# Window attention and two feed-forward layers: another hand-written order for the opening, and raw q and k pieces spaced wider

## The chip, the cores and the metric

The kernel runs on one core of one Trainium2 chip. The metric is the device time of one execution in microseconds (us), as the median of several runs; lower is better. Shares, waits and durations come from one execution that the hardware profiler took. The engines are PE (TensorE, with PEld for its weight loads), DVE (VectorE), ACT (ScalarE), POOL (GpSimd) and SP (SyncE, which issues most DMAs).

## The reference, cut to what matters

```python
# attention: batch 4, 8 heads, sequence 576, head size 64, a causal window of 64
scores = scale * np.matmul(q, k.transpose(0, 1, 3, 2))
mask = (rel >= 0) & (rel < 64)            # rel = row position - column position
attn = softmax(np.where(mask, scores, -1e9))
x = (attn @ v)                            # laid out as 2304 tokens x 512
h = np.maximum(np.maximum(x @ w1, x @ w2), x @ w3)   # 512 -> 768, three weights
x = h @ w_out                             # 768 -> 512
h = x @ w_in                              # 512 -> 2048
g = np.where(h >= 1, h, np.where(h <= -1, 0.0, (h + 1) ** 2 / 4))
out = g @ w2_out                          # 2048 -> 512
```

## The kernel before, in words

**The stages.** Attention and the first feed-forward product (stage A) run together, then come the second product (B), the third (C) and the fourth (D). Every fp32 matrix product of these layers is made of three passes over operands that are split into a high and a low part. Stages B to D use Strassen's seven products. The weights lie in memory as 64-bit words, from which two 32-bit halves are joined.

**Stage A.** The 2304 tokens are 9 blocks of 256. A product, named A0, A1 and so on, is one block times one 128-column piece of one of w1, w2, w3: 12 matmuls of 128x256 into one PSUM tile (`a_mm`, L427). `a_end` (L438, named D0, D1 and so on) takes the tile away: w1's on ACT, w2's and w3's with a maximum on DVE. After w3's in the second half of the columns, DVE makes sums (H) and SP stores `hq` (ST, `h_store` L456). There are 162 products. Before the 19th one, A12 to A17 take products of block 0 and block 1 in turn.

**Attention** goes by 36 groups g of 64 rows (`BL`), 9 to a batch. Its steps have short names, with n the group or, for loads and transposes of q and k, the pair of groups 2n and 2n+1:

- LQn, LKn: loads of q and k (`load`, L235), 256 KB each, or two halves where a batch ends. LVn: load of v (`vload`, L266).
- TQn, TKn: transposes on PE (`prep_t`, L282). CQn on ACT and CKn, the copies out of PSUM (`prep_c`, L287). 
- QKn: scores on PE. Rna, Rnb: mask and minimum on DVE (`red`, L342). Ena, Enb: exponentials on ACT (`ex`, L353). Sn: reciprocal on DVE (`norm`). Nn: scaling on POOL (`scale`, L371). PTn: transpose of the probabilities on PE (`ptr`). PCn: copy (`ptc`, L386). PVn: times v (`pv`, L393). VHn, VLn: high part on ACT and low part on DVE of the block's x (`values`, L405).

From group 18 on, except 26 and 27, q and k come in raw pieces (`raw_load`, L254): 16 pieces of 32 KB for q and 16 for k hold four groups, in rows of 32 numbers, and DVE transposes them.

**Weights of stage A** come in 9 pairs of 1 MB (LWn, `w_first` L638, `w_load` L165), two DMAs each, in 3 buffers `wst` (`NW`, L23). W1.n and W0.n are the two words on ACT (`w_word` L182, `w_lower` L199), SHn a shift on DVE (`w_upper`, L203), ADn the sum on DVE (`w_sum`, L207), HIn the high part (`w_high`, L211), LOna and LOnb the low parts on POOL (`w_low`, L214). Pair n holds the weights of A(2n) and A(2n+1) in the first 13 products. A `wst` buffer is free again after HIn and ADn. The decoded words have two buffers (`WT`, L24), held until LOnb.

**What sets the order.** Each engine and SP's queue work their instructions off in program order. Up to A17 that order is written out by hand in the string `SEQ` (L59), which `early` (L667) turns into steps. Steps before A0 stand in the order in which they are to go; later ones carry a place behind "@", counted in products. A star puts CQ, PC and HI on DVE and not on ACT; for CK it is the other way round (L665, L677). Steps from product 18 on and everything of the later groups get places from formulas (L689 to L716): a visit to two groups each 9 products, at place `vq`, with loads of q and k 13 products ahead of it (`LP - 4`), v at it, transposes 3 ahead. Raw pieces begin 28 products ahead (`RAWS`, L40), one each `RAWSTEP` of a product (L41, L702). The visits of groups 8, 10, 12 and 14 are at places 12.2, 18.2, 24.2 and 34.2. All places are sorted into one order (L803). PSUM tiles of TQ, TK and A share three buffers (L151).

```python
if g in pet:
    if g > g0:                                            # g0 = 8
        put(vq + LP - 4, load, g)
elif g in raws[::CH]:
    for z in range(32):
        put(vq + RAWS + RAWSTEP * z, raw_load, g, z)
put(vq, vload, g)
```

From place 14 on, a weight pair of the later stages is loaded, decoded, summed and stored each 6.2 products (`SLOTSTEP`, L55).

Of the kernel before, what the change touches and what calls it, by code (L numbers as in the profile page):

```python
# [37 lines left out]
STAGES = (-21, -9, -3, 0, 0.2, 1, 6, 9)  # L38
LP = -9
RAWS = -28  # L40
RAWSTEP = 0.4  # L41

# [12 lines left out]


SEQ = (  # L59
# [16 lines left out]
)  # L76
WS = 8

# [2 lines left out]
def kernel(ctx, tc, q, k, v, w1, w2, w3, wo1, wi2, wo2, out, hd, x2d, td, gd):  # L81
# [36 lines left out]
    N1 = max(n for _, n in blocks1)  # L118
# [508 lines left out]
    def put(at, fn, *args):  # L627
        order.append((at, len(order), fn, args))
# [60 lines left out]
    g0 = blocks1[PB][0] // BL  # L689
# [3 lines left out]
    for x, g1 in enumerate(range(g0, NG, 2)):  # L693
        vq, vt, vp = (visits[x + y] + 0.2 for y in range(3))
        for y in range(2):
            g = g1 + y
            if g in pet:
                if g > g0:
                    put(vq + LP - 4, load, g)
            elif g in raws[::CH]:  # L700
                for z in range(32):
                    put(vq + RAWS + RAWSTEP * z, raw_load, g, z)  # L702
            put(vq, vload, g)
            if g not in pet or g > g0:
                put(vq + STAGES[2], prep, g)
            if g > g0 + 1:
                put(vq + 0.02, qk, g)
                for z in range(2):
                    put(vq + RED[y] + z, red, g, (2 * z, 2 * z + 1))
                    put(vq + EXP[y] + z, ex, g, (2 * z, 2 * z + 1))  # L710
                put(vq + EXP[y] + 2, norm, g)
                put(vq + EXP[y] + 2, scale, g)
            put(vt + 0.01, ptr, g)
            put(vt + PTC[y], ptc, g)
            put(vp, pv, g)
        put(vp + 0.04, val, g1, 2)  # L716
# [365 lines left out]
```

## Time and profile before

| what | us |
|---|---|
| median of 3 runs | 772.27 (771.88 to 773.39) |
| the profiled execution, its own time | 770.42 |
| its span, first to last instruction | 768.6 |
| PE busy | 738.3 |
| DVE busy | 574.6 |
| ACT busy | 423.3 |
| POOL busy | 258.2 |

Two numbers on each engine are to be read together: its busy time, and what ended the idle time ahead of an instruction. PE's matmuls are counted busy at either level of its clock, so a matmul that takes twice as long is busy all that time; the granted clock stands in a column of its own. The mean granted clock over the span is 0.987 of full speed.

### The profile page before, as it was taken

The numbers are of one execution on the slowest core, as the hardware profiler recorded it, in microseconds if no ns is written. First come the engines' busy times: TensorE is split into PE (matmuls) and PEld (weight loads), VectorE is DVE, ScalarE is ACT, GpSimd is POOL, SyncE is SP. The second block draws the span as 40 slices with busy tenths as digits, with TensorE's granted clock in tenths as the row PEclk, the third lists the DMA queues.
The fourth block names the chain that finished last, engine by engine and source line by source line (L and its number), as shares of the span: only waits on it lengthen the run. The fifth ranks groups of instructions, "written<-read, shape, count | busy, mean of one in ns | idle before, by whom it ended". The sixth has DMA issues, their size and how long they took to land. (4 is left out here: it accounts for less than half of the span.)

```text
span 768.6 us, 17450 instructions
## 1 busy us (share of the span) xinstructions
PE 738.3 (96%) x6680; PEld 720.6 (94%) x6680; DVE 574.6 (75%) x1315; ACT 423.3 (55%) x806; POOL 258.2 (34%) x315
## 2 busy tenths in 40 slices
PE   5689999999999899999999999999999999999997
PEld 4578989999999799999999999999999999999997
DVE  4776767787786785677876778768888999988881
ACT  7865575556563553434547766767776434433330
POOL 2653395355535362300039442732269000000000
PEclk9798999999999999999999999999999999999999
DMA  9984989998999983797868653555456544544421
GB/s 247 288 232 115 232 193 259 252 326 206 257 248 278 332 256 121 229 296 227 246 185 286 203 146 122 201 188 196 162 199 190 170 138 144 167 126 123 130 83 55
DMA packets 221652, 154.75 MB, mean 201 GB/s; under 512 B 95233, under 2 KB 213633, under 8 KB 221569
## 3 DMA queue, kind: packets, MB, share of 16 engines
q1 hardware_dynamic: 191600, 110.91, 52.4%
q10 hardware_dynamic: 26384, 28.06, 10.4%
q0 software_dynamic: 3584, 14.68, 5.1%
q8 instruction: 52, 0.85, 0.5%
q14 instruction: 32, 0.25, 0.1%
HBM read 98.24 MB, written 55.38 MB: 200 GB/s over the span
## 5 line engine op out<-in xcount | busy, mean ns | idle before, releaser
L433 PE MATMUL ps<-xt,arena 128*128 128x256 f32 x1944 | 239.2, 284 | 8.3 <-DVE hq L450 3.5
L433 PEld LDWEIGHTS ps<-xt,arena 128*128 128x128 f32 x1944 | 233.3, 191 | 12.3 <-DVE hq L450 3.8
L125 ACT ACTIVATE side<-plain 128x1024 fp32r<-128x1024 f32 (+3 forms) x64 | 61.6, 978 | 56.9 <-DVE plain L504 36.8
L125 ACT ACTIVATE arena<-plain 128x1024 fp32r<-128x1024 f32 (+3 forms) x62 | 60.0, 977 | 35.7 <-DVE plain L504 25.8
L504 DVE TENSOR_TENSOR plain<-plain 128x256 f32<-128x256 f32 (+1 forms) x172 | 76.1, 459 | 4.7 <-DMA plain<-g_scratch 2.4
L128 DVE TENSOR_TENSOR side<-plain,side 128x1024 fp32r<-128x1024 f32 (+3 forms) x53 | 60.8, 1173 | 18.2 <-ACT side L125 18.2
L128 POOL TENSOR_TENSOR arena<-plain,arena 128x256 fp32r<-128x256 f32 (+1 forms) x65 | 54.6, 873 | 47.1 <-ACT arena L125 47.0
L128 POOL TENSOR_TENSOR side<-plain,side 128x256 fp32r<-128x256 f32 (+1 forms) x38 | 34.5, 942 | 101.6 <-ACT side L125 95.5
L125 ACT ACTIVATE ht<-ps 128x256 f32<-128x256 f32 x54 | 20.6, 382 | 79.8 <-PE ps L433 50.9
L360 ACT ACTIVATE sm<-sm,nm 128x128 f32<-128x128 f32 (+1 forms) x144 | 55.4, 392 | 15.4 <-DVE nm L348 14.7
L374 POOL TENSOR_TENSOR sm<-sm,rs 128x512 f32<-128x512 f32 (+1 forms) x36 | 37.4, 1041 | 57.6 <-DVE rs L369 50.8
L504 DVE TENSOR_TENSOR hq<-hq 128x128 f32<-128x128 f32 x108 | 55.4, 514 | 1.6
L450 DVE TENSOR_TENSOR ht<-ps,ht 128x256 f32<-128x256 f32 x54 | 22.7, 421 | 31.1 <-PE ps L433 17.0
L874 ACT ACTIVATE ut<-ut 128x288 f32<-128x288 f32 x64 | 43.9, 686 | 2.0
L128 DVE TENSOR_TENSOR arena<-plain,arena 128x1024 fp32r<-128x1024 f32 (+3 forms) x34 | 40.5, 1198 | 5.6 <-ACT arena L125 5.3
L450 DVE TENSOR_TENSOR hq<-ps,ht 128x256 f32<-128x256 f32 x54 | 22.5, 417 | 24.9 <-PE ps L433 19.4
L185 ACT ACTIVATE wst<-wst 128x1024 f32<-128x1024 f32 x28 | 32.1, 1147 | 14.1 <-DMA wst<-in_moe_w 7.3
L883 DVE SCALAR_TENSOR_TENSOR ut<-ut,evt 128x864 f32<-128x864 f32 x32 | 37.9, 1184 | 1.5 <-ACT ut L874 1.4
L128 POOL TENSOR_TENSOR arena<-wt,arena 128x512 fp32r<-128x512 f32 (+1 forms) x26 | 29.8, 1168 | 27.3 <-DVE wt L209 19.9
L504 POOL TENSOR_TENSOR wx<-wt 128x256 f32<-128x256 f32 x26 | 19.2, 740 | 57.7 <-DVE wt L197 50.0
L859 DVE TENSOR_TENSOR evt<-cc,evt 128x288 f32<-128x288 f32 x64 | 29.2, 456 | 8.4 <-PE cc L776 6.6
L125 ACT ACTIVATE evt<-ca 128x288 f32<-128x288 f32 x40 | 16.2, 405 | 34.0 <-PE ca L776 28.7
(170 smaller groups left out, 1779.5 us busy)
## 6 DMA issues: line engine op xcount, KB each, us to landing
g_scratch<-ut ACTq DMA_DIRECT2D x64, 288.0 KB, 3.1
plain<-g_scratch SPq DMA_DIRECT2D x36, 512.0 KB, 4.1
plain<-t_scratch SPq DMA_DIRECT2D x16, 896.0 KB, 5.3
h_scratch<-hq SPq DMA_DIRECT2D x27, 448.0 KB, 5.2
plain<-h_scratch SPq DMA_DIRECT2D x12, 1008.0 KB, 7.2
wst<-in_moe_w_out SPq DMA_DIRECT2D x22, 512.0 KB, 6.1
wst<-in_moe_w SPq DMA_DIRECT2D x18, 512.0 KB, 5.8
wst<-in_moe_w_in SPq DMA_DIRECT2D x16, 512.0 KB, 5.3
```

The costliest lines, as they stand in the source:

```text
L125: nc.scalar.activation(dst, src, AF.Copy, scale=scale)
L128: eng.tensor_tensor(dst, a, b, op=ALU.subtract)
L185: nc.scalar.activation(w.bitcast(F32), w.bitcast(F32), AF.Prelu, scale=2.0 ** (WS - 119), alpha=2.0 ** 32)
L360: nc.scalar.activation(sm[:, p, 0:W], sm[:, p, 0:W], AF.Exp, bias=d["nm"][:, p:p + 1], scale=-1.0, accum_out=ss[:, p:p + 1])
L374: nc.gpsimd.tensor_tensor(sm[:, :, 0:W], sm[:, :, 0:W], rs.unsqueeze(2).to_broadcast([P, NP, W]), op=ALU.mult)
L433: nc.tensor.matmul(ps[:, 0:n], w_col((w, f), wl, kt), xt[:, xl, kt, 0:n], start=(x == 0), stop=(x == len(passes) - 1))
L450: nc.vector.tensor_tensor(t[:, 0:n], ps[:, 0:n], part[j, f][:, 0:n], op=ALU.max)
L504: eng.tensor_tensor(o, a, b, op=op)
L859: nc.vector.tensor_tensor(o, a, b, op=ALU.add)
L874: nc.scalar.activation(o, o, AF.Square)
L883: nc.vector.scalar_tensor_tensor(o, o, 2.0 ** WS, x, op0=ALU.min, op1=ALU.max)
```

## The change

`SEQ` is replaced by another list of the same steps, with six more loads in it: LV8, LV9, LQ5, LK5, LQ6 and LK6, which the formulas gave places before. The formulas leave those six out now. In the list, LK4 stands ahead of A0 and not at place 8.25, LQ4, LV5 and LV6 behind A0, LW1 and LW2 further forward, and LW6 to LW8 at 5.78, 6.84 and 8.2, ahead of LV8, LQ5, LQ6, LK6 and LV9. W0.3 and W1.4 come ahead of A0; TQ4, CQ4, R6, R7b, E6a and E7a come behind it. CK0, CK3, CK4 go from ACT to DVE; PC0 and PC2 go from DVE to ACT, as do HI0, HI3 and HI8. `RAWSTEP` is 0.56 and not 0.4.

```diff
--- before.py
+++ after.py
@@ -38,7 +38,7 @@
 STAGES = (-21, -9, -3, 0, 0.2, 1, 6, 9)
 LP = -9
 RAWS = -28
-RAWSTEP = 0.4
+RAWSTEP = 0.56
 
 
 
@@ -57,22 +57,23 @@
 
 
 SEQ = (
-    "LQ0 LK0 TQ0 LQ1 CQ0 TK0 LK1 *CK0 TQ1 QK0 LK2 CQ1 QK1 R0a LQ2 TK1 E0a R0b R1a E0b TK2 LW0 CK1 E1a TQ2 S0 QK2 R1b "
-    "N0 CQ2 QK3 E1b R2a PT0 E2a R2b LV1 CK2 E2b *PC0 LV2 QK4 W0.0 S1 PV0 S2 LW1 N1 W1.0 R4a R3a N2 PT1 E3a R3b R4b "
-    "QK5 E3b SH0 E4b PT2 S3 LV3 *HI0 W0.1 AD0 LV4 W1.1 LQ3 *PC1 LO0a E4a *PC2 PV1 LK3 VH0 SH1 TQ3 N3 R5a LV5 HI1 TK3 "
-    "R5b LO0b S4 LW2 PT3 VH1 VL0 E5a VL1 PV2 N4 *PC3 CQ3 *CK3 AD1 PT4 VH2 E5b QK6 LQ4 VL2 LO1a W1.2 S5 PV3 R6a LW3 "
-    "W0.2 N5 TQ4 R6b QK7 E6a SH2 PT5 CQ4 LO1b R7a HI2 R7b LV6 AD2 E7a LW4 VH3 LO2a W1.3 VL3 "
-    "A0@0 E6b@0.19 SH3@0.33 E7b@0.74 LO2b@0.83 S6@0.9 A1@1 LW5@1.26 D0@1.29 S7@1.45 W1.4@1.56 N6@1.73 A2@2 PC4@2.33 "
-    "*HI3@2.47 W0.3@2.75 D1@2.98 N7@2.98 A3@3 D2@3.25 W0.4@3.3 LV7@3.3 AD3@3.42 PT6@3.58 W1.5@3.74 PV4@3.77 SH4@3.92 "
-    "A4@4 LW6@4.01 D3@4.32 *PC5@4.36 LO3a@4.36 PC6@4.59 A5@5 HI4@5.01 SH5@5.2 AD4@5.57 HI5@5.68 PT7@5.75 A6@6 "
-    "*PC7@6.21 LO3b@6.21 W1.6@6.23 LW7@6.31 D4@6.55 PV5@6.72 LO4a@6.86 D5@6.88 D6@6.92 A7@7 VH5@7.28 W0.5@7.55 "
-    "H5a@7.71 A8@8 LO4b@8.12 D7@8.24 LK4@8.25 W1.7@8.43 VL5@8.49 AD5@8.88 A9@9 W0.6@9.04 H5b@9.32 VH4@9.37 LW8@9.38 "
-    "TK4@9.44 D8@9.51 LO5a@9.51 D9@9.56 VL4@9.64 *CK4@9.71 PV6@9.83 SH6@9.91 A10@10 VH6@10.2 LO5b@10.2 HI6@10.4 "
-    "VL6@10.5 PV7@10.72 AD6@10.85 W1.8@10.94 A11@11 D10@11.36 W0.7@11.37 LO6a@11.43 QK8@11.54 D11@11.69 QK9@11.75 "
-    "VH7@11.78 R8a@11.89 A12@12 ST5@12 LO6b@12.01 VL7@12.1 E8a@12.24 R8b@12.39 E8b@12.84 SH7@12.9 A13@13 D12@13.39 "
-    "AD7@13.54 HI7@13.66 A14@14 H11a@14.4 D13@14.41 W0.8@14.68 LO7a@14.84 R9a@14.84 A15@15 R9b@15.29 E9a@15.44 "
-    "D14@15.6 LO7b@15.89 S8@15.9 E9b@15.98 A16@16 D15@16.28 H11b@16.79 A17@17 N8@17.23 D16@17.28 S9@17.58 SH8@17.96 "
-    "*HI8@17.98 AD8@17.98 D17@17.98 LO8a@17.98 LO8b@17.98 N9@17.98 ST11@18"
+    "LQ0 LK0 LQ1 LK1 LW0 LV1 TQ0 LV2 LK2 CQ0 TK0 LV3 LQ2 CK0 TQ1 LW1 QK0 CQ1 LW2 QK1 R0a LV4 TK1 E0a R0b R1a E0b CK1 "
+    "E1a S0 QK2 W1.0 R1b N0 QK3 E1b SH0 PT0 W0.0 S1 R3a N1 PC0 R2a TK2 R3b E3a AD0 PT1 E3b PV0 E2a S3 TQ2 *PC1 N3 VH0 "
+    "CK2 HI0 PV1 VL0 R2b CQ2 LO0a LW3 VH1 QK4 E2b LQ3 VL1 LO0b QK5 LK3 W1.1 S2 LK4 R4a W0.1 N2 R4b R5a E4b R5b PT2 "
+    "SH1 W0.2 PT3 AD1 E5b HI1 E4a LO1a LW4 *PC3 PC2 E5a S4 PV2 LO1b W1.2 S5 TQ3 N4 PV3 W0.3 SH2 TK3 CQ3 N5 TK4 VH2 "
+    "CK3 PT4 VH3 HI2 AD2 PT5 QK6 W1.3 QK7 VL3 LO2a LW5 VL2 W1.4 R7a "
+    "A0@0 LQ4@0.09 SH3@0.33 LV5@0.48 E7a@0.57 LO2b@0.82 R7b@0.82 A1@1 CK4@1.13 D0@1.28 HI3@1.55 AD3@1.72 A2@2 "
+    "W0.4@2.3 SH4@2.59 A3@3 E7b@3.06 D1@3.08 LO3a@3.08 D2@3.53 HI4@3.61 AD4@3.98 A4@4 D3@4.27 W1.5@4.48 LO3b@4.64 "
+    "S7@4.64 TQ4@4.75 D4@4.97 A5@5 LK5@5.01 CQ4@5.28 LV6@5.39 SH5@5.43 W0.5@5.71 LW6@5.78 N7@5.92 R6a@5.92 A6@6 "
+    "D5@6.28 LV7@6.45 E6a@6.47 R6b@6.58 LO4a@6.66 LW7@6.84 A7@7 HI5@7.02 AD5@7.56 D6@7.77 A8@8 E6b@8.01 D7@8.15 "
+    "LO4b@8.15 LW8@8.2 PC4@8.21 S6@8.26 *PC5@8.36 PV4@8.4 N6@8.46 D8@8.53 PV5@8.58 VH4@8.64 LO5a@8.72 PT6@8.77 "
+    "VL4@8.78 VH5@8.81 PT7@8.88 W1.6@8.91 VL5@8.96 A9@9 H5a@9.17 PC6@9.5 *PC7@9.6 LO5b@9.6 W0.6@9.92 A10@10 LV8@10.01 "
+    "LQ5@10.22 SH6@10.29 D9@10.39 LQ6@10.44 PV6@10.56 H5b@10.56 HI6@10.64 LK6@10.66 PV7@10.78 AD6@10.81 LV9@10.87 "
+    "A11@11 W1.7@11.07 D10@11.3 LO6a@11.38 VH6@11.5 QK8@11.56 W0.7@11.65 VL6@11.73 QK9@11.78 SH7@11.89 A12@12 ST5@12 "
+    "VH7@12.13 LO6b@12.29 R9a@12.29 HI7@12.42 VL7@12.59 D11@12.86 A13@13 AD7@13.16 D12@13.24 E9a@13.51 A14@14 "
+    "H11a@14.02 W1.8@14.06 LO7a@14.46 R9b@14.46 R8a@14.77 D13@14.83 A15@15 E8a@15.23 H11b@15.37 E9b@15.78 D14@15.81 "
+    "LO7b@15.81 A16@16 R8b@16.1 W0.8@16.33 S9@16.48 SH8@16.78 A17@17 E8b@17.03 D15@17.09 N9@17.09 D16@17.18 HI8@17.2 "
+    "AD8@17.32 D17@17.59 LO8a@17.63 S8@17.68 N8@17.92 ST11@18 LO8b@18.15"
 )
 WS = 8
 
@@ -695,12 +696,13 @@
         for y in range(2):
             g = g1 + y
             if g in pet:
-                if g > g0:
+                if g > g0 + 4:
                     put(vq + LP - 4, load, g)
             elif g in raws[::CH]:
                 for z in range(32):
                     put(vq + RAWS + RAWSTEP * z, raw_load, g, z)
-            put(vq, vload, g)
+            if g > g0 + 1:
+                put(vq, vload, g)
             if g not in pet or g > g0:
                 put(vq + STAGES[2], prep, g)
             if g > g0 + 1:
```

## Rows read from the trace of the kernel before

**Rows 1.** The page's part 1: busy time, share of the span, instructions.
```profile
PE 738.3 (96%) x6680; PEld 720.6 (94%) x6680; DVE 574.6 (75%) x1315; ACT 423.3 (55%) x806; POOL 258.2 (34%) x315
```

**Rows 2.** Windows: PE, PEld, DVE, ACT, POOL busy (instructions), granted clock, DMA share, GB/s.
```profile
0.00:10.00 10.00, 5.67 (x60) 4.44 (x64) 2.14 (x18) 4.85 (x14) 1.63 (x11) 1.00 0.89 217
10.00:20.00 10.00, 4.88 (x92) 3.38 (x92) 8.22 (x42) 9.61 (x33) 2.83 (x4) 1.00 1.19 272
20.00:30.00 10.00, 7.57 (x83) 6.11 (x84) 7.72 (x28) 6.91 (x21) 7.27 (x7) 0.66 1.01 261
...
40.00:50.00 10.00, 10.00 (x106) 9.57 (x105) 9.11 (x11) 7.93 (x11) 5.93 (x4) 1.00 0.69 205
50.00:60.00 10.00, 7.03 (x55) 6.33 (x54) 6.00 (x11) 5.18 (x9) 2.55 (x2) 0.76 1.00 285
...
250.00:260.00 10.00, 6.61 (x60) 6.48 (x62) 6.85 (x16) 3.80 (x12) 3.97 (x6) 0.83 1.06 308
```

**Rows 3.** Waits of PE, 0 to 150 us: total us, times, longest.
```profile
PE ps L433 <- ACT xt L125: 2.9, 1, 2.9
...
PE tp L285 <- DMA nat<-in_k: 2.2, 1, 2.2
...
PE ops L401 <- DVE xt L128: 0.8, 1, 0.8
```

**Rows 4.** PE's timeline, 25 to 110 us: start, us, what, [idle before <-releaser].
```profile
34.43 7.72 PE L433 MATMUL ps<-xt,arena 128*128 128x256 f32 x48 [2.94 <-ACT xt L125]
...
42.52 0.69 PE L401 MATMUL ops<-pt,vr 128*64 128x64 f32 x16
...
48.63 4.51 PE L433 MATMUL ps<-xt,arena 128*128 128x256 f32 x36
...
57.20 1.12 PE L401 MATMUL ops<-pt,vr 128*64 128x64 f32 x16 [0.80 <-DVE xt L128]
58.25 2.93 PE L433 MATMUL ps<-xt,arena 128*128 128x256 f32 x12
```

**Rows 5.** SP's timeline, 0 to 150 us: LW7, then LK4.
```profile
46.96 1.02 SPq L170 DMA_DIRECT2D wst<-in_moe_w  x2
48.02 1.88 SPq L249 DMA_DIRECT2D nat<-in_k  x2
```

**Rows 6.** DMA issues of 48 to 49 us: size, us to landing.
```profile
nat<-in_k SPq DMA_DIRECT2D x1, 128.0 KB, 6.6
```

**Rows 7.** Groups by form, 0 to 120 us: count | busy us, mean ns | idle before.
```profile
L360 ACT ACTIVATE sm<-sm,nm 128x128 f32<-128x128 f32 x56 | 21.8, 394 | 6.7 <-DVE nm L348 6.7
L374 POOL TENSOR_TENSOR sm<-sm,rs 128x512 f32<-128x512 f32 x13 | 14.8, 1142 | 15.0 <-DVE rs L369 10.5 <-DVE ss L368 4.4
...
L185 ACT ACTIVATE wst<-wst 128x1024 f32<-128x1024 f32 x12 | 13.8, 1150 | 7.3 <-DMA wst<-in_moe_w 7.3
...
L125 ACT ACTIVATE ht<-ps 128x256 f32<-128x256 f32 x14 | 5.3, 376 | 12.0 <-PE ps L433 12.0
...
L125 ACT ACTIVATE qt<-tp 128x512 f32<-128x512 f32 x8 | 4.7, 590 | 5.9 <-PE tp L285 5.8
```

**Rows 8.** Timeline, 25 to 62 us: a low part on POOL.
```profile
29.78 1.27 POOL L128 TENSOR_TENSOR arena<-wt,arena 128x512 fp32r<-128x512 f32 x1
```

**Rows 9.** Line 205 (SH), 30 to 62 us: duration ns minimum/median/maximum.
```profile
L205 DVE TENSOR_SCALAR wst<-wst x5: 685/1195/1543, 30.1 to 57.1; 128x1024 int32<-128x1024 int32 x5
```

**Rows 10.** PE's timeline, 240 to 300 us.
```profile
253.39 5.96 PE L433 MATMUL ps<-xt,arena 128*128 128x256 f32 x36 [3.45 <-DVE hq L450]
```

**Rows 11.** Line 457 (h_store): who waited for it, and landing min/median/max.
```profile
  DVE hq L450: 5.4, 1
...
DMA to landing us min/median/max: 3.3/5.2/9.6
```

**Rows 12.** SP's timeline, 225 to 262 us: raw k pieces, then the store.
```profile
237.21 4.88 SPq L260 DMA_DIRECT2D raw<-in_k  x7
...
243.20 0.56 SPq L457 DMA_DIRECT2D h_scratch<-hq  x1
```

## The prediction, made before the run

> **What bounds the kernel now.** I read four views, from the coarse to the fine. The engines' busy times come first: PE is busy for 738.3 of 768.6 us [rows 1], so a change that leaves the matmuls alone can win only PE's 30 us of idle time and what a lower clock costs. The windows say where that lies [rows 2]: in the first 30 us PE is busy 5.67, 4.88 and 7.57 us of each 10, from 40 to 50 all the time, from 50 to 60 only 7.03 at a granted clock of 0.76, and from 250 to 260 only 6.61 at 0.83. The waits name what ended the gaps [rows 3]: the first product waited 2.9 us for ACT; a transpose waited 2.2 us for a k load, and the PV after it 0.8 us. The timeline prices them [rows 4]: A0 starts at 34.43, and its first four products take 7.72 us where 36 matmuls, three products, take 4.51 at full clock, so part of them ran at the lower level (1.2 and not 2.4 GHz), right after 2.94 idle us. The same happens after the k load: the next product takes 2.93 us and not 1.50, and a PV 1.12 and not 0.69.
>
> **The k load's stall: 5.7 us.** In the order of before LK4 stands at place 8.25, behind LW7, and TK4 at 9.44. SP issued LW7 at 46.96 and LK4 at 48.02 [rows 5]; that kind of load took 6.6 us to land [rows 6], so at 54.6 or later, while PE had come to TK4 at 53.1 (48.63 + 4.51 [rows 4]). The idle time is 2.2 + 0.8 = 3.0 us, which is what the window of 50 to 60 lacks. The lower clock costs 2.93 - 1.50 = 1.4 for the product and 1.12 - 0.69 = 0.4 each for the transpose and two PVs, together 2.7. In the new list LK4 stands ahead of LW4 and TK4 ahead of A0, so this goes: -5.7 us. What is late next is TQ4, at place 4.75. Its LQ4 stands behind LW5, which waits for HI2 and AD2, issued about when A0 starts; 6.6 us of landing against 5 products of 1.50, 7.5 us. It holds by about 1 us. LW6 to LW8 have no k load behind them that PE needs soon, and each is issued when HI and AD of three pairs before are done.
>
> **Where A0 starts: no change, between 2.7 us won and 1.5 lost.** Two chains set it. ACT, ahead of VH3: W0.3 is new (+1.15, a word of the same size [rows 7]), one copy of 128x512 less (5 CQ and 2 CK become 4 CQ and 2 PC, -0.59), four exponentials less (-1.6); HI0 comes and HI2 goes behind VH3. That is 1.0 us less, so 33.4 if ACT waits as long as before. DMA and PE: up to LK4 the queue carries four weight pairs (4.2 MB) and 13 loads of q, k and v (3.4 MB), 7.6 MB. At 217, 272 and 261 GB/s [rows 2] the first 30 us moved 7.5, so LK4 lands at 30.4. Behind it on PE stand TK4, PT4, PT5, QK6 and QK7 ahead of A0. The nearest row is a PV: 0.69 or, at the lower clock, 1.12. Five take 3.4 or 5.6, so A0 starts at 33.8 or 35.9. I take 34.4, as before, with the clock of its first products as before (it cost 7.72 - 6.01 = 1.7). Ends: 1.0 + 1.7 won, 1.5 lost.
>
> **Products 0 to 18: +0.8 us, between 0 and 2.2.** Six loads that the formulas placed are now in the list, within one product of their old place (LK5, LQ6, LK6) or 1 to 5 products from it (LQ5, LV8, LV9). All come at least four products ahead of their use: no cost, hidden behind products that need none of them. ACT carries more: HI3 and two PCs, less CK4. Up to VH7, which A13 needs, it has 12 weight steps of 1.15 (W1 three, W0 four, HI five), 8 exponentials of 0.39, 4 D and 4 VH of 0.38, and 3 copies of 0.59: 21.7 us [rows 7]. PE takes 13 products of 1.50 and eight small steps of 0.69 to 1.12, some 25 us. It fits, with 3 us to spare. DVE was busy 9.11 of 10 us at 40 to 50 [rows 2] and stays near that; it loses HI3 and one PC and gets CK4. The one place I find late is PT8 at 18.21: S8 stands behind D17 (17.59), so N8 on POOL starts after A17. D17 and S8, some 0.4 each by the row of D, and 1.14 for N8 make 1.9, against 1.50 for A18 in between: 0.4 us of waiting. LO8a (1.27 [rows 8]) can come in front of N8: 1.7. With 0.5 more for a second POOL step, 2.2 is the upper end; I take 0.8, nearer to the chain without it.
>
> A row of DVE speaks against this list: SH took 685 ns at the least and 1543 at the most [rows 9], the longest starting while POOL ran a low part of 1.27 us [rows 8]. The Trainium skill ("SBUF — State Buffer", SBUF: two separate sides) says why: VectorE and GpSimd share a pair of ports, whichever starts first holds it for its whole instruction, and the other waits. By that every one of the five SH up to A13 could take 0.69 + 1.27 = 1.95; by the row's median they take 1.20, which I use. The difference is a rival below.
>
> **Raw pieces 0.56 apart: -3.5 us, between 0 and -4.9.** The pieces' number, bytes and queue stay; only their places among SP's other work move. At 253.39 PE had idled 3.45 us for DVE's `hq` [rows 10], DVE 5.4 us for a store of `hq` that took 9.6 us to land, the longest of 27 [rows 11]. SP issued it at 243.20, right behind raw pieces that took it 4.88 us for seven, 0.70 each [rows 12]. The store's place is 102 (block 5 begins at 90, 5 for its sixth product, 7 for the store). The raw pieces of groups 32 to 35 begin at 115.2 - 28 = 87.2: at 0.4 apart all 32 stand ahead of the store (the last at 99.6), at 0.56 only 27. Five fewer are 3.5 us earlier, just what PE's gap needs. The clock behind it cost 5.96 - 4.51 = 1.45 more. I take the idle time and leave the clock out, because the next store (place 108) then has those five pieces ahead of it and is needed sooner. For groups 18, 22 and 28 the last piece moves 5 products back, to 41.6, 59.6 and 86.6, against transposes at 49.2, 67.2 and 94.2: 7.6 products remain, over 11 us, more than the 9.6 of the longest landing of a store; no cost.
>
> **The sum.** -5.7 + 0 + 0.8 - 3.5 = -8.4, so 762.0 against the profiled execution's own 770.42. The median of the runs, 772.27, is 1.85 above it; with that, **763.9**. Its own range, with not all ends at once, is 759 to 768.
>
> **Rivals.**
>
> 1. **The late stall stays.** The opening wins its 5.7, but the store at 102 is still late or the one at 108 takes its place: DMA is busy all of 250 to 260 (share 1.06 [rows 2]), and fewer pieces ahead on SP don't make room there. For: the landing of 9.6 us, twice the median. Against: the queue's order does improve. -4.9: 767.4.
> 2. **The shared ports.** Five SH at 1.95 and not 1.20 add 3.8 us to DVE. At 9.11 of 10 it has 2.2 to spare in 25 us, so A13 waits 1.6 for VL7. If the clock then falls as it did after 2.9 idle us, 2.7 more. -6.8 to -4.1: 765.5 to 768.2. The Trainium skill's rule named above would do this; the median of the row speaks against all five being hit.
> 3. **The order changes nothing.** The wait for LK4 becomes one for LQ4 behind LW5, of the same price, and the late stall stays: +0.8 alone, 773.1. Against: LQ4's 1 us of margin.
> 4. **Slower: HI0 holds up the k loads.** LW3 takes LW0's buffer, which HI0 frees, and LQ3, LK3 and LK4 stand behind it on SP. HI0 is on ACT now, behind VH0, so behind PV0, which stands behind TK2 on PE, and LK2 now lands behind LW0, LV1 and LV2. Ahead of LW3 stand 5.8 MB, which at the rates of rows 2 keep DMA busy to 23.4, so it decides when HI0 ends after some 20 us; from there each us delays A0 by one. Against: by ACT's order HI0 ends near 18. Price for 7 us late: +7, A0's clock low for four products more (+1.7), and with the late stall kept -5.7 + 0.8: +3.8, so 776.1.
>
> **How the numbers follow.** Chances: the forecast 0.52, rival 1 0.20, rival 2 0.08, rival 3 0.07, rival 4 0.13. 0.2% is 1.5 us, about what a measurement of this kernel can tell from no change. The forecast, rivals 1 and 2 are faster by more: 0.80. Rival 3 is the same: 0.07. Rival 4 is slower: 0.13. The range runs from the forecast's lower end, 759.0, over rivals 1 and 2 to 770.5, where mixtures with a late A0 end; what lies outside is rivals 3 and 4.
>
> **What would show it.** Right: in the windows of 50 to 60 us PE is busy throughout at full clock; TK4 has no wait for a k load after A0; the 19th product starts some 5 us earlier; near 250 us DVE waits for no store. Wrong: a wait of TQ4 for its q load, of A13 for DVE, of SP for HI0 ahead of LW3 with DMA's share falling at 20 to 30 us, or A0 after 36. If A0 starts after 36, the part on A0 was wrong; if the wait for a store is found at 108's place or later, the part on the raw pieces was.

## The result, and the profile after

The kernel after takes **763.76 us** (median of 4 runs, 763.57 to 764.97), the kernel before 772.16 beside it (4 runs, 771.88 to 773.39): a ratio of 0.9891, 95% interval 0.9874 to 0.9909. 763.9 was forecast, so the number holds. Its terms do not all hold. The profiled execution of after takes 763.64 us with a span of 761.9, 6.8 less than that of before; the sum in the prediction was 8.4. The 1.85 us that I added, because the profiled execution of before was that much under its median, have no counterpart: the one of after is 0.12 under its own.

The page's part 1 of after, the busy times [rows 1]:

```profile
PE 735.6 (97%) x6680; PEld 718.5 (94%) x6680; DVE 573.6 (75%) x1313; ACT 425.7 (56%) x808; POOL 259.8 (34%) x315
```

Windows of after, columns as in [rows 2]:

```profile
20.00:30.00 10.00, 4.11 (x57) 3.35 (x53) 6.88 (x25) 8.86 (x26) 5.03 (x5) 0.62 1.01 253
...
50.00:60.00 10.00, 10.00 (x136) 9.54 (x133) 8.13 (x20) 9.24 (x17) 5.41 (x4) 1.00 0.95 264
60.00:70.00 10.00, 8.53 (x72) 8.05 (x71) 7.06 (x25) 6.58 (x19) 3.57 (x4) 1.00 0.85 240
70.00:80.00 10.00, 6.88 (x67) 5.97 (x67) 2.32 (x11) 2.15 (x7) 3.40 (x3) 0.83 1.01 260
...
250.00:260.00 10.00, 10.00 (x132) 9.46 (x131) 8.47 (x29) 6.67 (x19) 4.19 (x6) 1.00 1.05 344
```

Both holes that the prediction read in [rows 2], 50 to 60 and 250 to 260, are full at full clock. A new one is there: 70 to 80, PE 6.88 and a clock of 0.83. PE's timeline of after says what stands around A0 and in the new hole (start, us, what, [idle before <-releaser]; [rows 4] answers to it):

```profile
28.78 1.12 PE L402 MATMUL ops<-pt,vr 128*64 128x64 f32 x16 [3.78 <-ACT pt L126]
...
35.28 7.33 PE L434 MATMUL ps<-xt,arena 128*128 128x256 f32 x60
42.86 0.63 PE L286 MATMUL tp<-ident,nat 128*128 128x128 f32 x4 [0.25 <-DMA nat<-in_q]
...
57.43 5.86 PE L434 MATMUL ps<-xt,arena 128*128 128x256 f32 x48
...
65.86 4.47 PE L434 MATMUL ps<-xt,arena 128*128 128x256 f32 x36 [0.79 <-DVE kring L296]
73.45 1.94 PE L384 MATMUL pps<-ident,sm 128*128 128x128 f32 x8 [3.12 <-POOL sm L375]
75.32 1.87 PE L338 MATMUL sps<-kring,qt 64*64 64x128 f32 x32
77.12 4.47 PE L434 MATMUL ps<-xt,arena 128*128 128x256 f32 x36
```

A0 starts at 35.28, 0.85 later than before, but the five products from there on take 7.33 us, so they run at full clock from the first; before, four took 7.72 [rows 4]. A12 (the group of 48 matmuls) starts at 57.43, and in the trace of before, on the same view, at 64.59:

```profile
64.59 5.86 PE L433 MATMUL ps<-xt,arena 128*128 128x256 f32 x48
```

From A0 to A12 that is 22.15 us against 30.16: 8.0 won. The group of A16 to A18, the 17th to the 19th product, starts 7.2 us earlier than before (65.86 and 73.02). Then PE waits 3.12 us for PT8's scaling N8, and PT8 and QK at the lower clock take 1.94 and 1.87. What is left of the lead at the 20th product, A19, the group at 77.12, is 2.2 us (79.3 before). It stays so up to about 246 us. There the second gain comes: product 114 starts at 248.9 and not at 256.1, so 4.9 us more.

What went on around N8, in the timeline of all engines of after:

```profile
69.69 0.42 DVE L451 TENSOR_TENSOR hq<-ps,ht 128x256 f32<-128x256 f32 x1
69.92 2.49 POOL L129 TENSOR_TENSOR arena<-wt,arena 128x512 fp32r<-128x512 f32 x2 [1.47 <-DVE wt L210]
70.02 1.19 DVE L369 TENSOR_SCALAR ss<-ss 128x4 f32<-128x4 f32 x1
...
71.24 0.18 DVE L370 RECIPROCAL rs<-ss 128x4 f32<-128x4 f32 x1
72.36 1.04 POOL L375 TENSOR_TENSOR sm<-sm,rs 128x512 f32<-128x512 f32 x1
```

D17 ends at 70.11. POOL runs two low parts, LO8a and LO8b, from 69.92 to 72.41; S8 (the TENSOR_SCALAR on 128x4) takes 1.19 us beside the first, and N8 starts only behind the second.

The late stall is gone from the waits of PE, and this is SP's timeline of after around the store of place 102 [rows 12], and what the DMA view says of that store [rows 11]:

```profile
234.27 2.33 SPq L261 DMA_DIRECT2D raw<-in_k  x2
236.70 0.81 SPq L458 DMA_DIRECT2D h_scratch<-hq  x1
237.56 3.99 SPq L261 DMA_DIRECT2D raw<-in_k  x5
```
```profile
h_scratch<-hq SPq DMA_DIRECT2D x1, 448.0 KB, 5.5
```

Five raw pieces now stand behind the store, as worked out, and it lands in 5.5 us and not 9.6.

### The profile page after: what moved, and what is told of

Its sections match the earlier page's. It is cut to its first block, busy times and chain, and to the rows that moved or that the text cites. A ratio compares the mean times of both kernels' runs of the same rounds, so it can differ in the third digit from the quotient of the medians.

```text
span 761.9 us, 17462 instructions
## 1 busy us (share of the span) xinstructions
PE 735.6 (97%) x6680; PEld 718.5 (94%) x6680; DVE 573.6 (75%) x1313; ACT 425.7 (56%) x808; POOL 259.8 (34%) x315
## 4 chain that ended last, share of the span: by engine, by line
PE 44%; DVE 2%; issue 1%; DMA 1%; POOL 1%; ACT 1%; ACTq 0%; DVEq 0%
PE dz L1007 7%; PE dx L1007 7%; PE dy L1007 7%; PE cc L778 6%; PE ce L778 6%; PE ca L778 6%; PE dw L1007 3%; PE cb L778 3%; DMA plain<-t_scratch 1%; POOL arena L129 1%; DVE left L129 1%; DVE evt L861 0%; DVE plain L505 0%; ACT side L126 0%; DVE side L129 0%
## 5 line engine op out<-in xcount | busy, mean ns | idle before, releaser
L434 PE MATMUL ps<-xt,arena 128*128 128x256 f32 x1944 | 233.7, 280 | 1.8 <-DVE ht L451 1.1
L434 PEld LDWEIGHTS ps<-xt,arena 128*128 128x128 f32 x1944 | 228.8, 188 | 5.1 <-issue 1.8
L505 DVE TENSOR_TENSOR hq<-hq 128x128 f32<-128x128 f32 x108 | 52.8, 490 | 1.6
L129 POOL TENSOR_TENSOR arena<-wt,arena 128x512 fp32r<-128x512 f32 (+1 forms) x26 | 32.6, 1280 | 14.9 <-ACT arena L126 6.4
L349 DVE CUSTOM_DVE_ANT_0 sm<-sps,maskA 128x128 f32<-128x128 f32 (+1 forms) x112 | 26.1, 275 | 13.0 <-PE sps L338 12.7
```

What stands on the lines that cost most here:

```text
L129: eng.tensor_tensor(dst, a, b, op=ALU.subtract)
L434: nc.tensor.matmul(ps[:, 0:n], w_col((w, f), wl, kt), xt[:, xl, kt, 0:n], start=(x == 0), stop=(x == len(passes) - 1))
L505: eng.tensor_tensor(o, a, b, op=op)
```

## The experiments

Ten kernels ran, in three jobs, each beside the kernel before (medians 772.34, 772.36, 772.22). In these jobs runs of one kernel differ by several us, so effects of 1 or 2 us are read from the traces, and the medians only as ratios. All ten compute everything.

**e1: the new list with the old spacing.**

```diff
-RAWSTEP = 0.56
+RAWSTEP = 0.4
```

> The changed kernel with RAWSTEP back at 0.4. Theory (the late stall hung on the raw pieces ahead of the store of place 102): with all 32 pieces ahead of it again, DVE waits near 250 us for a store of hq, PE idles some 3.5 us and runs at the lower clock behind it, so 4 to 5 us more than the changed kernel: 767.5 to 769. Rival (the new opening moved the stall away): no such wait, 763 to 764.5.

Measured: 764.64 (761.87 to 768.48, 6 runs), ratio 0.9904 [0.9868, 0.9941]. Its profiled run took 767.49, 3.9 more than that of after, and has the late stall. Waits of PE in e1, from 150 us on, and its store on SP:

```profile
PE ps L434 <- DVE hq L451: 2.5, 1, 2.5
```
```profile
241.03 0.57 SPq L458 DMA_DIRECT2D h_scratch<-hq  x1
```

The store took 9.4 us to land. So in the traced run the late stall is back, as the theory has it, and the opening keeps its gain (A0 to A12 take 22.66 us). The medians do not say so: 764.64 is nearest to the rival's range, and the spacing is worth only 0.9 us on top of the new list, inside the spread. The traced execution is the second longest of six that lie 6.6 us apart; how many of the others have the stall is not known.

**e2: the old list with the new spacing.**

```diff
-RAWSTEP = 0.4
+RAWSTEP = 0.56
```

> The kernel before with RAWSTEP 0.56 alone. Theory: the opening's rows are those of before (TK4's stall of 2.2 and 0.8 us stays), and the stall near 250 us goes with its clock, 4 to 5 us less than before: 767 to 768.5. Rival: the stall stays, 771.5 to 773.

Measured: 766.39 (764.67 to 767.99, 6), ratio 0.9918 [0.9887, 0.9950]; span 764.4, 4.2 less than before. No wait of PE from 150 to 300 us is left; the one of TK4 in the opening stays (2.7 us). Store issued at 239.84, landed in 5.1. The spacing takes the late stall away by itself. But the two gains do not add up by the medians: the list alone (e1, 0.9904) and the spacing alone (0.9918) would make 0.982, and after has 0.9891.

**e5: spacing 0.46 in the old list, all 32 pieces still ahead of the store.**

```diff
-RAWSTEP = 0.4
+RAWSTEP = 0.46
```

> The kernel before with RAWSTEP 0.46: the pieces are spread, but the last of groups 32 to 35 stands at 87.2 + 31 x 0.46 = 101.5, so all 32 are still ahead of the store at 102. Theory (the number of pieces ahead on SP's queue decides): the store is issued as late as before, the stall stays, 771 to 773. Rival (a thinner stream gives the store a faster landing): the stall shrinks or goes, 767 to 770.

Measured: 768.2 (765.73 to 772.19, 12), ratio 0.9950 [0.9927, 0.9973]; no late stall. SP's timeline of e5, and its store in the DMA view:

```profile
242.21 0.92 SPq L260 DMA_DIRECT2D raw<-in_k  x2
243.23 0.56 SPq L457 DMA_DIRECT2D h_scratch<-hq  x1
```
```profile
h_scratch<-hq SPq DMA_DIRECT2D x1, 448.0 KB, 4.9
```

The store is issued at the same time as before (243.20 [rows 12]), behind all 32 pieces, and lands in half the time, 4.7 us sooner, which alone is more than PE's 3.45. The rival won: the number of pieces ahead of the store is not by itself what made it late. Its opening was some 2 us slower, so the store came 1.9 us ahead of the start of product 108 and not 0.4 behind it; a part of the margin comes from that. The pair of weights ahead of the store, 1 MB, moved too: SP issued it 0.9 us ahead of the store in before (242.27) and e1 (240.08), 2.5 in e5 (240.73) and 3.4 in after (233.34). Windows of before, after, e1 and e5 from 240 to 245 us, in this order (columns as in [rows 2]):

```profile
240.00:245.00 5.00, 5.00 (x67) 4.66 (x65) 2.94 (x17) 2.44 (x8) 3.92 (x6) 1.00 0.73 116
```
```profile
240.00:245.00 5.00, 5.00 (x45) 5.00 (x45) 2.67 (x15) 3.24 (x13) 1.82 (x4) 1.00 1.13 336
```
```profile
240.00:245.00 5.00, 5.00 (x43) 5.00 (x44) 2.71 (x17) 2.03 (x9) 2.62 (x5) 1.00 0.83 198
```
```profile
240.00:245.00 5.00, 5.00 (x87) 4.39 (x86) 3.47 (x10) 2.53 (x7) 2.58 (x4) 1.00 0.84 253
```

Where the store is late, before and e1, DMA moves 116 and 198 GB/s in this stretch; where it is in time, 336 and 253. But the stretch holds only the first 1.8 us of the store's flight in before. Over the whole flight DMA moves 303 GB/s in before (243.20 to 252.80) and 338 in e5 (243.23 to 248.13), so it is not slow there: 2.9 MB pass before the store has landed, and 1.7 in e5. What is slow comes ahead of it, as the DMA view of before from 242.2 to 242.5 us shows:

```profile
DMA packets 198, 0.02 MB, mean 81 GB/s; under 512 B 198, under 2 KB 198, under 8 KB 198
```

My reading is that closely spaced raw pieces hold up the weights behind them, and that the store comes behind both. No run moves the weights alone, so this is not shown.

**e6: the old spacing, that store alone 3.6 places earlier.**

```diff
-put(at + 7, h_store, args[0], args[1] - 3)
+put(at + (3.4 if args == (5, 3, 2) else 7), h_store, args[0], args[1] - 3)
```

> The kernel before with RAWSTEP 0.4, and one store alone moved: that of block 5's first hq from place 102 to 98.4, so that three raw pieces and one weight pair that stood ahead of it stand behind it. Theory (SP's queue order): the store is issued 2 to 4 us earlier, DVE's wait of 5.4 us shrinks to 1 to 3 and PE's 3.5 us go, 767 to 769. Rival (DMA's load alone sets the landing, wherever the store stands): the wait stays, 771 to 773.

Measured: 775.13 (769.77 to 779.85, 12), ratio 1.0041 [1.0008, 1.0074]: slower, which neither side expected. From the opening on, which the edit does not touch, PE in this trace is 3.2 us later than in that of before (A12 at 67.82 and 64.59); that is 3.2 of the 4.7 us between the two traced runs, and it is taken off where times are compared here. The store is issued 2.5 us earlier (243.94), lands in 3.9 us, and DVE waits for no store; so far the theory holds, and the rival is out. But the weight pair behind it is issued 2.1 us later (247.64, 242.27 before), ACT waits for it, and A's copy stands behind that on ACT. ACT's timeline of e6, and PE's:

```profile
255.72 1.10 ACT L185 ACTIVATE wst<-wst 128x1024 f32<-128x1024 f32 x1 [6.92 <-DMA wst<-in_moe_w_out]
...
259.29 0.36 ACT L125 ACTIVATE ht<-ps 128x256 f32<-128x256 f32 x1
```
```profile
259.70 2.71 PE L433 MATMUL ps<-xt,arena 128*128 128x256 f32 x11 [5.14 <-ACT ht L125]
```

In the trace of before the same copy comes just as late, while PE waits for `hq` until 253.39 [rows 10]:

```profile
253.06 0.36 ACT L125 ACTIVATE ht<-ps 128x256 f32<-128x256 f32 x1
```

So a wait for the weights lay under the one for the store. Moving the store alone hands the lateness on to the weights; with the pieces spaced wider, SP issues both earlier against PE's work.

**e3: the old list, LK4 ahead of LW4, all else in place.**

```diff
-AD2 E7a LW4 VH3
+AD2 E7a LK4 LW4 VH3
-LK4@8.25
```

> The kernel before with one step moved: LK4 from place 8.25 to ahead of LW4, before A0. Theory (LK4 behind LW7 was the cause of the stall): TK4 waits for no k load, the window of 50 to 60 us is full but for what the next late thing takes; by the prediction's price 5.7 us less, 766 to 768 (the late stall stays). Rival (the weights are as late as LK4): PE waits in the same place for a low part or a buffer, 769 to 772.

Measured: 770.06 (767.37 to 774.95, 12), ratio 0.9971 [0.9944, 0.9998]; A0 at 35.15 and A12 at 65.20, so 30.05 us between them and 30.16 before; the rival's range has the median. TK4 waits no longer, but PE's timeline of e3 has a gap of the same size in the same place (before [rows 4]: 2.18 and 0.80):

```profile
57.38 1.12 PE L401 MATMUL ops<-pt,vr 128*64 128x64 f32 x16 [3.00 <-DVE xt L128]
58.43 2.93 PE L433 MATMUL ps<-xt,arena 128*128 128x256 f32 x12
```

This PV6 needs VL4 on DVE, that needs VH4 on ACT, and VH4 (place 9.37) stands behind W1.7 (8.43), which waits for LW7. Waits of e3, 0 to 150 us:

```profile
ACT wst L185 <- DMA wst<-in_moe_w: 6.9, 5, 3.1
```

The mechanism that the prediction named was one of two, one on top of the other.

**e8 and e9: W1.7 behind VH4, with LK4 early (e8) and alone (e9).** e8 has e3's edit too.

```diff
-W1.7@8.43
+W1.7@9.63
```

> The kernel before with LK4 ahead of A0, as in the last experiment on it, and W1.7 on ACT moved from place 8.43 to behind VH4 (9.63). Theory (two waits lay on top of each other: TK4 for LK4, and PV6 for VL4, whose VH4 stood behind W1.7 on ACT, which waits for LW7's landing): with both out of the way the idle time between 50 and 60 us and the lower clock behind it go, and the 13th product starts 5 to 6 us earlier, counted from the first: 766 to 767.5. Rival (a third step waits for LW7 as well, such as A10's low part): under 2 us earlier, 769 to 772.

> The kernel before with W1.7 alone moved behind VH4, and LK4 where it was. Theory (either wait alone keeps the gap): TK4 still waits 2 to 3 us for its k load, the 13th product starts as late after the first as before, within 1.5 us: 770.5 to 773. Rival (the wait on ACT was the real one and LK4's lay beside it): the gap goes, 766 to 768.

Measured: e8 767.77 (766.03 to 769.19, 7), ratio 0.9944 [0.9922, 0.9966]; A0 at 35.01, A12 at 60.15, 25.14 us, so 5.0 won. e9 770.89 (763.01 to 775.19, 12), ratio 0.9953 [0.9922, 0.9984]; A0 at 34.79, A12 at 63.08, 28.29, so 1.9 won, a little more than the 1.5 that the theory allowed, TK4 still waiting 2.21 us. PE's timeline of e8, the PV that waited 3.00 in e3:

```profile
54.90 0.69 PE L401 MATMUL ops<-pt,vr 128*64 128x64 f32 x16 [1.08 <-DVE xt L128]
55.52 1.67 PE L433 MATMUL ps<-xt,arena 128*128 128x256 f32 x12
```

Each edit alone won 0.1 and 1.9 us, both together 5.0: the gap goes but for 1.08 us, and its lower clock with it, only where both waits go. The traces of e2, e5 and e6, whose opening is that of before, have 30.57, 30.61 and 32.22 us from A0 to A12, so the 5.0 are far outside their spread and the 1.9 hardly. The late stall stays in e8 (4.5 us of waiting for `hq`). The list of after makes both edits in its own way: TK4 stands ahead of A0, and VH4 and VH5 (8.64, 8.81) ahead of W1.6 (8.91) and W1.7 (11.07).

**e4: S8 and N8 forward, ahead of D17 and of LO8a, in the kernel after.**

```diff
-S8@17.68 N8@17.92
+S8@17.1 N8@17.12
```

> The changed kernel with S8 and N8 moved from 17.68 and 17.92 to 17.10 and 17.12, ahead of D16, AD8, D17 on DVE and of LO8a and LO8b on POOL. Theory (PT8 waits for N8 because S8 stands behind D17 and POOL does two low parts first): the 3.12 us of idle time ahead of PT8 go, and the lower clock of the 16 instructions behind it (0.90 and 0.77 us), 4.8 less: 758 to 760. Rival (PT8 then waits for N9, for PC or for another step as long): 762 to 764.

Measured: 759.69 (757.68 to 761.33, 6), ratio 0.9834 [0.9808, 0.9861]. In PE's timeline of e4 the wait is gone, and PT8 takes 1.04 and not 1.94:

```profile
67.31 4.47 PE L434 MATMUL ps<-xt,arena 128*128 128x256 f32 x36 [0.78 <-DVE kring L296]
71.61 1.04 PE L384 MATMUL pps<-ident,sm 128*128 128x128 f32 x8
72.58 1.10 PE L338 MATMUL sps<-kring,qt 64*64 64x128 f32 x32
73.61 4.51 PE L434 MATMUL ps<-xt,arena 128*128 128x256 f32 x36
```

From A16 to the 20th product 6.30 us pass, in after 11.26: 5.0 us that the new list had lost.

**e10: e4 with D14 forward as well.** D14 is what TK5's copy waited behind.

```diff
-D14@15.81
+D14@15.1
```

> The changed kernel with S8 and N8 moved as in the earlier experiment, and D14 also moved from 15.81 to 15.1, ahead of the transposes of pair 5. Theory (TK5 and A16 wait 0.7 and 0.8 us because only one of the three PSUM buffers is free in program order while A14 and A15 have not been taken away): TK5 then takes A14's buffer and both waits go, 1 to 1.5 us less than with S8 and N8 alone, whose median was 759.7: 758 to 759. Rival (CQ5 and CK5 are waited for in any case): 759.3 to 760.

Measured: 758.55 (757.69 to 760.58, 6), ratio 0.9824 [0.9798, 0.9850]. The wait of 0.69 us between TQ5 and TK5 is gone and PT8 waits 0.42 again; A0 to A16 take 29.8 us and 31.2 in e4. It is the fastest kernel that ran; the 1.1 us to e4 are within the spread.

**e7: PC2 on DVE, in the kernel after.** PE's longest wait ahead of A0 but for the one for the first load, 3.78 us, is for PC2 on ACT.

```diff
-*PC3 PC2 E5a
+*PC3 *PC2 E5a
```

> The changed kernel with PC2 on DVE, as before, and not on ACT. Theory (PV2 waits 3.78 us for PC2 on ACT, PE's clock falls, and the steps up to A0 run at the lower clock): PV2 goes 2 to 3 us earlier, the gap and its clock shrink, A0 starts at 33.5 to 34.5 and not at 35.3: 762 to 763.3. Rival (A0 waits for LK4's landing and ACT anyway): A0 at 35 to 36, 763.5 to 764.5.

Measured: 763.6 (761.77 to 765.16, 6), ratio 0.9884 [0.9858, 0.9910], as after. PE's timeline of e7:

```profile
27.37 0.78 PE L402 MATMUL ops<-pt,vr 128*64 128x64 f32 x16 [3.01 <-DVE pt L391]
29.22 1.11 PE L286 MATMUL tp<-ident,nat 128*128 128x128 f32 x4 [1.07 <-DMA nat<-in_q]
```

PV2 is 1.4 us earlier, TQ3 then waits for its q load, and A0 starts at 35.85. The rival won: behind the wait for ACT stood one for a load.

## Why the prediction was right, and where its terms were not

- **The k load's stall (-5.7).** The size is right, the cause half right. A0 to A12 is 8.0 us shorter: 1.7 for A0's first products at full clock (the term below), some 0.6 for PVs and PTs of two groups that now follow each other (a pair takes 1.15 and 1.09 in PE's timeline of after, where single ones took 0.69 [rows 4] and 0.60), and the rest, 5.7, is the gap. The step that failed is the reading of [rows 4] that put all 3.0 us of idle time, PV6's 0.80 with it, down to LK4. e3 shows that without LK4's wait VL4 ends PE's idle time at the same place; e8 shows that W1.7's place is the other half. I got the sum because the new list moves VH4 too, which the prediction did not see.
- **TQ4 holds by about 1 us.** It waited 0.25 us for LQ4: so little margin as was worked out, and a little less. Rival 3 was near.
- **Where A0 starts (0, from -2.7 to +1.5).** It started 0.85 late, inside the ends, and its clock won 1.7, which I had left as before: together -0.85 and not 0. PE worked from 28.78 on without a break, first at the lower clock, and A0 found it at full clock. The upper end of the row's estimate, 35.9 with five steps at the lower clock, was the nearer one.
- **Products 0 to 18 (+0.8, from 0 to 2.2).** This is the term that was wrong: 5.0 by e4, beyond its upper end. The place was named (PT8 behind N8 behind S8 behind D17), three parts were too small. POOL ran both low parts ahead of N8 and not one, 1.25 us more: the list has LO8b behind N8 (18.15, 17.92), but from place 12 on the program ties only the other engines to the list. S8 took 1.19 and not 0.4, held up by POOL; the trace of before had a row for this, an S of 1.02 us at 27.38 beside a low part from 27.10 to 28.37. And the lower clock behind the 3.12 us of idle time, 0.90 + 0.77, was left out, though [rows 4] show the same behind 2.94.
- **Raw pieces (-3.5, from 0 to -4.9).** Its upper end came in the traces of before and after: 4.9 us, the 3.45 of waiting and the 1.45 of clock. I had left out the clock, expecting the next store to fall late; none did. The step "Five fewer are 3.5 us earlier, just what PE's gap needs" failed as the whole cause. In after the store is issued 3.8 us ahead of product 108 and not 0.4 behind it, so it is earlier as worked out; but e5 has all pieces ahead of the store and no stall, and e6 has the store in time and a stall of 5.1 us for the weights. What fits all is that closely spaced pieces make late whatever comes behind them, the weights as well as the store; whether by the queue's order or by the rate of their small rows was not tried apart and stays open. So does the size on top of the new list: 3.6 us of e1's 3.9 arise here by the traces, 0.9 by the medians.
- **The sum.** Of -8.4, the traces give -7.1 up to product 114: -1.4 on the raw pieces, -0.85 on A0 and -0.6 on the pairs were better than forecast, +4.2 at PT8 worse. Some 0.3 us are lost behind it, so -6.8. The 1.85 added for the median of before made up for the rest. The number is so near by compensation of errors, not by exact terms.
- **The rivals.** Rival 1 did not come in after; e1 and e8 show what it looks like. Rival 2 did not come at A13: the eight SH up to 62 us have a median of 694 ns, one reaches 1520. The rule behind it, the Trainium skill's on the ports that VectorE and GpSimd share ("SBUF — State Buffer", SBUF: two separate sides), is borne out by the S steps: up to 80 us six of the ten in after began while POOL ran a low part, and each ended within 0.04 us of its end, S8 after 1.19 us and the longest after 1.27, where the shortest of the ten took 0.17. I had priced it on SH alone. Rival 4 did not come: SP issued LW3 at 19.00 and LK4 by 29.4, and LK4 landed in 4.7 us.

## What to carry to other kernels

Where two idle times stand close behind each other with different releasers, work out for each what PE would wait for if the other were gone; the gap may belong to both, and moving one alone does little (0.1 and 1.9 us here, against 5.0). Of a short step late in an in-order chain, count everything that can run ahead of it on each engine that it passes, with what another engine can hold up (S8 here), and add what the clock cost behind the nearest idle time in the trace (1.4 to 2.7 us here). A transfer that lands late is not always too far back in its queue: look at what DMA moved ahead of it, and at what is next to be late if it alone is moved.

## What the runs showed of the hardware that was not expected

A DVE instruction on 128x4 elements took 1.19 us while POOL ran a low part of some 1.25 us, and ended when that ended (71.21 against about 71.17); in e4, where POOL was in the last 0.2 us of N9, the same S8 took 0.25. So an operation's own size does not bound what POOL can cost it. And a store of 448 KB, issued at 243.2 in two traces, landed in 9.6 and in 4.9 us, with raw pieces 0.4 and 0.46 of a product apart: a small change of spacing halved it, and moved the weights ahead of the store with it.
